# Loading the first two chunks of X by columns, and running the first piece of K ahead of the other turns

## The chip, the cores and the metric

The kernel runs on one core of a Trainium2 chip. Times are device microseconds (us) of that core. The engines are TensorE (PE; its weight loads are listed as PEld), VectorE (DVE), ScalarE (ACT), GpSimd (POOL) and SyncE (SP). DMAs are issued here from SP and from ACT. A time without a profile is the median over several executions; a profile is one execution, with times counted from its first instruction.

## What is computed

X has 2048 rows (S) of 640 features (D), in bfloat16. The result mixes two blocks with a gate per row:

```python
g = _sigmoid((x * gate_w).sum(-1, keepdims=True))
a = _A_ref(x, A_wqkv, A_wo)               # linear attention, 32 heads of 20
b = _B_ref(x, B_w1, B_w2, B_w3, B_w4)     # layernorm, gelu, shifts, MLP of 1728
return g * a + (1 - g) * b
```

The part that the change touches is the start of the attention block: `k = x @ wqkv[:, 640:1280]`, then `phi(k)`, for all rows, and with it the gate's sum `x * gate_w`, which the kernel computes as one more column of the same matrix product.

## The kernel before

X is cut into 16 chunks of 128 rows, its 640 features into 5 pieces (`dc`) of 128. A matmul of K for a chunk needs X transposed: `xT[:, dc, rows]` is the stationary operand and `wk_sb[:, dc, ...]`, one fifth of K's weights, the moving one. K's 640 outputs are taken in two halves (`hf`) of 320, each in its own bank of a PSUM pair, and each sums over the five `dc`. Half 1 has 321 columns: the last is the gate's, so that the gate's logit comes out beside K. So a chunk takes ten matmuls of K.

The schedule is written out by hand: each engine runs its instructions in the order in which the program lists them. The kernel's body is a sequence of stages: K for all chunks, Q, the products of phi(K) with X, two layer norms and the MLP. The change is in the first of them.

From chunk 2 on, X arrives already transposed by seven transposing loads that SP issues (L125). For chunks 0 and 1 that would come too late. They are loaded as they are (`load_x`, L122), and PE turns them itself: a matmul of a 128x128 block of `x_sb` with the identity (`turn`, L217) writes the turned block to PSUM, and a copy (L219), on DVE for pieces 0 and 1 and on ACT for pieces 2 to 4, brings it to `xT`.

The order of the issues at the start is: on SP chunk 0, chunk 1, K's weights 1 and 3, then the transposing loads; on ACT the gate's weights (`g5`, L131), then K's weights 0, 2 and 4 (L128), and then a table load and a first Exp (L208).

PE begins with filler matmuls (`warmup`, L204) on a constant, whose results nobody reads. The gate's weights arrive as five rows (`g5`), are copied into a zeroed square (`g5z`, L207), turned by one matmul of 5 columns (L210) and cast into the column `wk_sb[:, :, D]` (L212). Then come chunk 0's five turns, a filler, chunk 1's turns of pieces 1 and 0, K's piece 0 for chunk 0 (two matmuls, L191), chunk 1's other three turns, K's piece 0 for chunk 1, and the other four pieces of K for both chunks, sixteen matmuls. After each chunk ACT copies the gate's logit (L195) and takes the exponential (L183), and DVE ends phi (L184, L185). Chunks 2 to 15 follow with ten matmuls each.

Four PSUM pairs exist: `warm` and `tp` take the turns, and `kps[0]` and `kps[1]` the K sums of chunks 0 and 1. Fillers write to the second bank of `kps[1]`.

Of the kernel before, what the change touches and what calls it, by code (L numbers as in the profile page):

```python
# [7 lines left out]
ACT = mybir.ActivationFunctionType  # L8
# [8 lines left out]
def kernel(  # L17
# [13 lines left out]
    nc = tc.nc  # L31
    P = 128
    S, D = A_x.shape[1], A_x.shape[2]
# [3 lines left out]
    TS = 512  # L37
    NT = S // TS
    CPT = TS // P
    DC = D // P  # L40
# [12 lines left out]
    x2 = A_x.rearrange("b s d -> (b s) d")  # L53
# [14 lines left out]
    def pair():  # L68
        return ps.tile([P, 2, 512], F32, name="pp")


    x_sb = const.tile([P, NCH, D + 16], BF16)
# [15 lines left out]
    ident = const.tile([P, P], BF16)  # L88
    g5 = const.tile([DC, P], BF16)
    g5z = const.tile([P, P], BF16)  # L90
# [7 lines left out]
    gate = const.tile([P, NCH], F32)  # L98
# [12 lines left out]
    wk_sb = st1.tile([P, DC, D + 16], BF16)  # L111
    gT = wk_sb
    xT = st1.tile([P, DC, S], BF16)
# [5 lines left out]
    sp, aq, gq = nc.sync, nc.scalar, nc.gpsimd  # L119

    def load_x(c0, c1, q=sp):
        q.dma_start(x_sb[:, c0:c1, 0:D], x2[c0 * P:c1 * P, :].rearrange("(c p) d -> p c d", p=P))  # L122

    def load_xT(c0, c1):
        sp.dma_start_transpose(xT[:, :, c0 * P:c1 * P], x2[c0 * P:c1 * P, :])  # L125

    def load_wk(q, dc):
        q.dma_start(wk_sb[:, dc, 0:D], A_wqkv[dc * P:(dc + 1) * P, D:2 * D])  # L128

    load_x(0, 1)  # L130
    aq.dma_start(g5[:], gate_w.rearrange("(c p) -> c p", p=P))  # L131
    load_x(1, 2)
    load_wk(aq, 0)
    load_wk(sp, 1)
    load_wk(aq, 2)
    load_wk(sp, 3)
# [1 line left out]
    for c0, c1 in ((2, 3), (3, 4), (4, 6), (6, 8), (8, 10), (10, 12), (12, 16)):  # L138
        load_xT(c0, c1)
# [44 lines left out]
        nc.vector.tensor_scalar(e[:, 0:n], e[:, 0:n], 1.0, 1e-6, op0=ALU.min, op1=ALU.add)  # L184
        nc.vector.scalar_tensor_tensor(dst, src, 0.0, ev, op0=ALU.max, op1=ALU.add)  # L185

    def k_mm(pt, c, dcs, first=0, last=DC - 1):
        for dc in dcs:
            for hf in range(2):
                n = HD + hf  # L190
                nc.tensor.matmul(pt[:, hf, 0:n], lhsT=xT[:, dc, c * P:(c + 1) * P],  # L191
                                 rhs=wk_sb[:, dc, hf * HD:hf * HD + n], start=(dc == first), stop=(dc == last))
# [5 lines left out]
    warm, tp = pair(), pair()  # L198
    kps = [pair(), pair()]
    one = nc.const_aps.tensor(1.0, (P, TS), BF16)  # L200

    def warmup(n, w=TS, pt=kps[1]):
        for i in range(n):
            nc.tensor.matmul(pt[:, 1, 0:w], lhsT=one[:, 0:P], rhs=one[:, 0:w], start=True, stop=True)  # L204

    nc.vector.memset(g5z[:], 0.0)
    nc.vector.tensor_copy(g5z[0:DC, :], g5[:])  # L207
    nc.scalar.activation(gate[:, 0:1], one[:, 0:1], ACT.Exp)  # L208
    warmup(5)
    nc.tensor.matmul(kps[0][:, 0, 0:DC], lhsT=g5z[:], rhs=ident[:, 0:DC], start=True, stop=True)  # L210
    warmup(1, P)
    nc.vector.tensor_copy(wk_sb[:, :, D], kps[0][:, 0, 0:DC])  # L212

    def turn(c, dcs, pt, copy):
        a, n = min(dcs), len(dcs)
        for dc in dcs:
            nc.tensor.matmul(pt[:, 0, (dc - a) * P:(dc - a + 1) * P], lhsT=x_sb[:, c, dc * P:(dc + 1) * P],  # L217
                             rhs=ident[:], start=True, stop=True)
        copy(xT[:, a:a + n, c * P:(c + 1) * P], pt[:, 0, 0:n * P].rearrange("p (c s) -> p c s", c=n))  # L219

    turn(0, (1, 0), tp, nc.vector.tensor_copy)
    turn(0, (2, 3, 4), warm, nc.scalar.copy)
    warmup(1, TS)
    turn(1, (1, 0), tp, nc.vector.tensor_copy)
    k_mm(kps[0], 0, (0,))
    turn(1, (2, 3, 4), warm, nc.scalar.copy)
    k_mm(kps[1], 1, (0,))
    for dc in range(1, DC):
        for c in range(2):
            k_mm(kps[c], c, (dc,))  # L230
    for c in range(2):
        k_evac(kps[c], c)
    for c in range(2, NCH):
        pt = pair()
# [515 lines left out]
```

## Time and profile before

| what | us |
|---|---|
| median of 3 runs | 261.5 (261.31 to 261.77) |
| the profiled execution | 260.77 |
| its span, first to last instruction | 259.1 |
| PE busy | 254.2 (98%) |
| DVE busy | 147.6 (57%) |
| ACT busy | 108.0 (42%) |
| POOL busy | 32.5 (13%) |
| first filler on PE | 0.83 |
| first turn of X on PE | 3.19 |
| first matmul of K on PE | 4.54 |

Matmuls overlap each other: one starts while the one ahead of it is still draining. So a row's busy time and mean duration are longer than the time that a matmul adds, and the difference between the starts of two neighbours is the better measure. The brackets at the end of a timeline row tell how long the engine was idle ahead of it, and what ended that.

### The profile page before, as it was taken

The numbers are of one execution on the slowest core, as the hardware profiler recorded it, in microseconds if no ns is written. First come the engines' busy times: TensorE is split into PE (matmuls) and PEld (weight loads), VectorE is DVE, ScalarE is ACT, GpSimd is POOL, SyncE is SP. The second block draws the span as 40 slices with busy tenths as digits, with TensorE's granted clock in tenths as the row PEclk, the third lists the DMA queues.
The fourth block names the chain that finished last, engine by engine and source line by source line (L and its number), as shares of the span: only waits on it lengthen the run. The fifth ranks groups of instructions, "written<-read, shape, count | busy, mean of one in ns | idle before, by whom it ended". The sixth has DMA issues, their size and how long they took to land.

```text
span 259.1 us, 4189 instructions
## 1 busy us (share of the span) xinstructions
PE 254.2 (98%) x1624; PEld 150.1 (58%) x1647; DVE 147.6 (57%) x274; ACT 108.0 (42%) x168; POOL 32.5 (13%) x86
## 2 busy tenths in 40 slices
PE   8999999999999999999999999999999999999995
PEld 4777555688854644565464566464565555465553
DVE  2588778799999987687300497500288600125132
ACT  3555544375797447431352323343321343342100
POOL 4000040023411230041000131000132000000000
PEclk9999999999999999999999999999999999999999
DMA  7999998015571887943011023212022411211011
GB/s 198 213 186 371 347 265 280 7 34 123 126 116 39 131 163 218 315 122 76 3 41 41 20 65 84 78 32 50 20 53 72 101 23 41 59 29 59 17 52 52
DMA packets 57358, 27.98 MB, mean 108 GB/s; under 512 B 45394, under 2 KB 56442, under 8 KB 57338
## 3 DMA queue, kind: packets, MB, share of 16 engines
q1 hardware_dynamic: 56896, 27.22, 42.4%
q10 hardware_dynamic: 442, 0.49, 0.5%
q8 instruction: 13, 0.21, 0.4%
q14 instruction: 7, 0.06, 0.1%
HBM read 12.86 MB, written 3.47 MB: 63 GB/s over the span
## 4 chain that ended last, share of the span: by engine, by line
PE 98%; issue 1%; DVE 0%
PE pp L572 21%; PE pp L611 16%; PE pp L191 9%; PE pp L522 8%; PE pp L341 8%; PE pp L553 8%; PE pp L396 8%; PE pp L243 8%; PE pp L647 5%; PE pp L204 1%; PE pp L582 1%; PE pp L603 1%; PE pp L217 0%; PE pp L452 0%; PE pp L429 0%
## 5 line engine op out<-in xcount | busy, mean ns | idle before, releaser
L572 PE MATMUL pp<-lnxT,w_sb 128*128 128x512 bf16 x249 | 59.8, 379 | 0.6
L574 ACT ACTIVATE h<-pp 128x1024 bf16<-128x1024 f32 (+1 forms) x28 | 26.9, 962 | 56.0 <-PE pp L572 56.0
L611 PE MATMUL pp<-h,w_sb 128*128 128x512 bf16 (+1 forms) x228 | 42.4, 343 | 0.3
L572 PEld LDWEIGHTS <-w_sb 128*128 128x128 bf16 x260 | 25.2, 98 | 26.9
L525 DVE TENSOR_TENSOR x<-pp,x_sb 128x640 f32<-128x640 f32 x16 | 13.1, 816 | 41.0 <-PE pp L522 41.0
L611 PEld LDWEIGHTS <-w_sb 128*128 128x128 bf16 x234 | 22.7, 98 | 19.5 <-issue 1.0
L183 ACT ACTIVATE e<-pp 128x640 bf16<-128x640 f32 (+1 forms) x26 | 21.4, 827 | 9.6 <-PE pp L243 9.6
L304 POOL TENSOR_SCALAR rstd<-mv 128x1 f32<-128x1 f32 (+2 forms) x22 | 9.1, 415 | 127.9 <-DVE mv L310 126.9
L559 DVE SCALAR_TENSOR_TENSOR x<-pp,gate,x 128x640 f32<-128x640 f32 x16 | 14.1, 882 | 18.2 <-PE pp L553 12.6
L553 PE MATMUL pp<-m_sb,pqT 128*128 128x320 bf16 x160 | 24.3, 299 | 0.0
L522 PE MATMUL pp<-w_sb,hsT 128*128 128x320 bf16 x160 | 23.9, 299 | 0.0
L191 PE MATMUL pp<-wk_sb,xT 128*128 128x320 bf16 (+1 forms) x160 | 22.6, 303 | 0.0
L341 PE MATMUL pp<-x_sb,pk 128*128 128x320 bf16 (+1 forms) x160 | 22.0, 300 | 0.0
L243 PE MATMUL pp<-xT,hsT 128*128 128x512 bf16 x98 | 21.6, 379 | 0.1
L341 PEld LDWEIGHTS <-pk 128*128 128x128 bf16 x160 | 18.8, 117 | 3.2
L522 PEld LDWEIGHTS <-hsT 128*128 128x128 bf16 x160 | 15.6, 98 | 8.3 <-issue 0.4
L553 PEld LDWEIGHTS <-pqT 128*128 128x128 bf16 x160 | 15.7, 98 | 7.7
L624 DVE SCALAR_TENSOR_TENSOR oc<-pqT,omg,x 128x640 bf16<-128x640 bf16 x12 | 10.5, 878 | 16.7 <-DMA pqT<-hx 16.7
L191 PEld LDWEIGHTS <-xT 128*128 128x128 bf16 x160 | 15.8, 100 | 6.1
L396 PE MATMUL pp<-lnxT,w_sb 128*128 128x512 bf16 x77 | 17.9, 379 | 0.2
L243 PEld LDWEIGHTS <-hsT 128*128 128x128 bf16 x100 | 11.8, 118 | 9.7
L305 POOL TENSOR_TENSOR rstd<-rstd,mhalf 128x1 f32<-128x1 f32 (+2 forms) x22 | 16.7, 761 | 1.8
(93 smaller groups left out, 248.8 us busy)
## 6 DMA issues: line engine op xcount, KB each, us to landing
x_sb<-in_A_x_dram SPq DMA_DIRECT2D x1, 2240.0 KB
out_dram<-oc SPq DMA_DIRECT2D x14, 160.0 KB, 2.0
w_sb<-in_B_w_dram SPq DMA_DIRECT2D x1, 2160.0 KB, 17.0
w_sb<-in_B_w_dram SPq DMA_DIRECT2D x1, 2080.0 KB, 8.6
hsT<-in_A_wqkv_dram SPq DMA_DIRECT2D x1, 800.0 KB, 6.1
m_sb<-in_A_wqkv_dram SPq DMA_DIRECT2D x1, 800.0 KB, 12.1
w_sb<-in_B_w_dram SPq DMA_DIRECT2D x1, 800.0 KB, 11.5
m_sb<-m_dram SPq DMA_DIRECT2D x1, 800.0 KB, 4.3
```

The costliest lines, as they stand in the source:

```text
L183: nc.scalar.activation(ev, src, ACT.Exp)
L191: nc.tensor.matmul(pt[:, hf, 0:n], lhsT=xT[:, dc, c * P:(c + 1) * P], rhs=wk_sb[:, dc, hf * HD:hf * HD + n], start=(dc == first), stop=(dc ...
L243: nc.tensor.matmul(pt[:, t % 2, :], lhsT=wq_sb[:, dc, :].rearrange("p (m j) -> p j m", j=DC)[:, j], rhs=xT[:, dc, t * TS:(t + 1) * TS], st ...
L305: nc.gpsimd.tensor_tensor(out_ap, out_ap, mhalf[:, 0:out_ap.shape[1]], op=ALU.pow)
L341: nc.tensor.matmul(pt[:, hf, 0:HD + hf], lhsT=w, rhs=x_sb[:, c, hf * HD:(hf + 1) * HD + hf], start=(c == 0), stop=(c == NCH - 1))
L396: nc.tensor.matmul(pt[:, i, :], lhsT=w, rhs=lnxT[t][:, dc, :], start=(dc == 0), stop=(dc == DC - 1))
L522: nc.tensor.matmul(pt[:, hf, 0:HD], lhsT=hsT[:, fc, 2 + c * P:2 + (c + 1) * P], rhs=w2_sb[:, fc, hf * HD:(hf + 1) * HD], start=(fc == 0), ...
L553: nc.tensor.matmul(pt[:, hf, 0:HD], lhsT=pqT[:, j, c * P:(c + 1) * P], rhs=m_sb[:, j, hf * HD:(hf + 1) * HD], start=(j == 0), stop=(j == D ...
L559: nc.vector.scalar_tensor_tensor(x1, pt[:, :, 0:HD], gate[:, c:c + 1], x1, op0=ALU.mult, op1=ALU.add)
L572: nc.tensor.matmul(pt[:, k, :], lhsT=w3_sb[:, dc, fc * P:(fc + 1) * P], rhs=lnT[:, dc, :], start=(dc == 0), stop=(dc == DC - 1))
L574: nc.scalar.activation(h2[:, 2 * i * TS:(2 * i + n) * TS], pt[:].rearrange("p h e -> p (h e)")[:, 0:n * TS], ACT.Gelu_apprx_tanh)
L611: nc.tensor.matmul(dst, lhsT=w4_sb[:, fc, d * P:(d + 1) * P], rhs=st[t]["h2"][:, fc * TS + a:fc * TS + b], start=False, stop=(fc == FF - 1))
```

## The change

Chunks 0 and 1 of X are no longer loaded one after the other. A first transfer on SP brings features 0 to 127 of both chunks (64 KB), and a second one, on ACT, features 128 to 639 of both (256 KB). K's weights 0 move from ACT to SP, behind the first transfer.

PE's order follows: after four fillers (five before) it turns piece 0 of both chunks, runs two fillers, then half 0 of K's piece 0 for both chunks. The gate's weights are now turned behind that, into `warm` and not `kps[0]`, and g5z is copied behind the first turns' copy. Then come the turns of piece 1 of both chunks, half 1 of K's piece 0, the turns of pieces 2 to 4 of chunk 0 (copied by ACT) and of chunk 1 (now copied by DVE, through `tp`). The other sixteen K matmuls keep their order. The turns and the K matmuls are as many as before, and so are the DMAs.

```diff
+    def load_x01(q, a, b):
+        q.dma_start(x_sb[:, 0:2, a:b], x2[0:2 * P, a:b].rearrange("(c p) d -> p c d", p=P))
...
-    load_x(0, 1)
+    load_x01(sp, 0, P)
     aq.dma_start(g5[:], gate_w.rearrange("(c p) -> c p", p=P))
-    load_x(1, 2)
-    load_wk(aq, 0)
+    load_wk(sp, 0)
+    load_x01(aq, P, D)
     load_wk(sp, 1)
     load_wk(aq, 2)
     load_wk(sp, 3)
...
-    def k_mm(pt, c, dcs, first=0, last=DC - 1):
+    def k_mm(pt, c, dcs, hfs=(0, 1), first=0, last=DC - 1):
         for dc in dcs:
-            for hf in range(2):
+            for hf in hfs:
...
     nc.vector.memset(g5z[:], 0.0)
+    nc.scalar.activation(gate[:, 0:1], one[:, 0:1], ACT.Exp)
+    warmup(4)
+
+    def turn_mm(cs, dcs, pt):
+        for i, (c, dc) in enumerate([(c, dc) for dc in dcs for c in cs]):
+            nc.tensor.matmul(pt[:, 0, i * P:(i + 1) * P], lhsT=x_sb[:, c, dc * P:(dc + 1) * P],
+                             rhs=ident[:], start=True, stop=True)
+
+    def turn_copy(cs, dcs, pt, copy):
+        a, d, m, n = min(cs), min(dcs), len(cs), len(dcs)
+        copy(xT[:, d:d + n, a * P:(a + m) * P], pt[:, 0, 0:m * n * P].rearrange("p (d s) -> p d s", d=n))
+
+    turn_mm((0, 1), (0,), tp)
+    turn_copy((0, 1), (0,), tp, nc.vector.tensor_copy)
+    warmup(1)
+    warmup(1, 2 * P)
     nc.vector.tensor_copy(g5z[0:DC, :], g5[:])
-    nc.scalar.activation(gate[:, 0:1], one[:, 0:1], ACT.Exp)
-    warmup(5)
-    nc.tensor.matmul(kps[0][:, 0, 0:DC], lhsT=g5z[:], rhs=ident[:, 0:DC], start=True, stop=True)
-    warmup(1, P)
-    nc.vector.tensor_copy(wk_sb[:, :, D], kps[0][:, 0, 0:DC])
...
-    turn(0, (1, 0), tp, nc.vector.tensor_copy)
-    turn(0, (2, 3, 4), warm, nc.scalar.copy)
-    warmup(1, TS)
-    turn(1, (1, 0), tp, nc.vector.tensor_copy)
-    k_mm(kps[0], 0, (0,))
-    turn(1, (2, 3, 4), warm, nc.scalar.copy)
-    k_mm(kps[1], 1, (0,))
+    for c in range(2):
+        k_mm(kps[c], c, (0,), (0,))
+    nc.tensor.matmul(warm[:, 0, 0:DC], lhsT=g5z[:], rhs=ident[:, 0:DC], start=True, stop=True)
+    nc.vector.tensor_copy(wk_sb[:, :, D], warm[:, 0, 0:DC])
+    turn_mm((0, 1), (1,), tp)
+    turn_copy((0, 1), (1,), tp, nc.vector.tensor_copy)
+    for c in range(2):
+        k_mm(kps[c], c, (0,), (1,))
+    turn_mm((0,), (2, 3, 4), warm)
+    turn_copy((0,), (2, 3, 4), warm, nc.scalar.copy)
+    turn_mm((1,), (2, 3, 4), tp)
+    turn_copy((1,), (2, 3, 4), tp, nc.vector.tensor_copy)
     for dc in range(1, DC):
```

## The prediction, on record before the result

> **What bounds the kernel now.** First the page's busy table and its chain that ended last.
>
> ```profile
> PE 254.2 (98%) x1624; PEld 150.1 (58%) x1647; DVE 147.6 (57%) x274; ACT 108.0 (42%) x168; POOL 32.5 (13%) x86
> ...
> PE 98%; issue 1%; DVE 0%
> ```
>
> TensorE (PE) is busy from end to end. So a change at the front is worth what it moves the moment at which PE starts chunk 2 of K; from there the stream is the same. Second, the chain in order of time, for the front alone.
>
> ```profile
> 0.83 2.29 PE pp L204 x5
> 3.12 0.14 PE pp L210
> 3.27 0.13 PE pp L204
> 3.40 0.53 PE pp L217 x5
> 3.93 0.43 PE pp L204
> 4.36 0.39 PE pp L217 x2
> 4.75 0.53 PE pp L191 x2
> 5.28 0.32 PE pp L217 x3
> 5.60 21.69 PE pp L191 x158
> ```
>
> L204 is filler, L217 the turns of X, L191 the matmuls of K. Chunks 0 and 1 need 10 turns and 20 K matmuls. Third, how long these take, from the timeline of PE in small windows.
>
> ```profile
> 5.08 0.53 PE L217 MATMUL pp<-ident,x_sb 128*128 128x128 bf16 x3
> 5.39 0.47 PE L191 MATMUL pp<-wk_sb,xT 128*128 128x320 bf16 x1
> ...
> 5.39 1.05 PE L191 MATMUL pp<-wk_sb,xT 128*128 128x320 bf16 x5
> ...
> 6.01 2.34 PE L191 MATMUL pp<-wk_sb,xT 128*128 128x321 bf16 x16
> ```
>
> Spacing counts, not duration. Before about 5.8 us two K matmuls take 0.53 us (4.54 to 5.08), 0.267 each, and three turns 0.32, 0.107 each. From 6.01 sixteen K matmuls cover 2.34 less the last one's tail (0.30 long, spaced 0.136): 0.136 each. So PE runs at half speed until about 5.8 us and at full speed behind it, though the page's PEclk row says 9 throughout and so doesn't show this. Chunk 2's first K matmul starts 16 x 0.136 behind 5.88, at 8.06 us: the mark that the change must move.
>
> Fourth, what the front waits for: the answers for the transfers in small windows, the vector engine's (DVE's) timeline, and the tile view of x_sb.
>
> ```profile
> x_sb<-in_A_x_dram SPq DMA_DIRECT2D x1, 160.0 KB, 2.2
> ...
> x_sb<-in_A_x_dram SPq DMA_DIRECT2D x1, 160.0 KB, 3.1
> wk_sb<-in_A_wqkv_dram ACTq DMA_DIRECT2D x1, 160.0 KB, 3.1
> ```
>
> ```profile
> 2.66 0.36 DVE L207 COPY g5z<-g 5x128 bf16<-5x128 bf16 x1 [1.67 <-DMA g<-in_gate_w_dram]
> 3.30 0.18 DVE L212 CAST wk_sb<-pp 128x5 bf16<-128x5 f32 x1 [0.28 <-PE pp L210]
> 3.65 0.42 DVE L219 CAST xT<-pp 128x256 bf16<-128x256 f32 x1 [0.16 <-PE pp L217]
> ```
>
> ```profile
>   DMA x_sb<-in_A_x_dram: 0.6, 1
> ```
>
> Chunk 0 of X, issued at 0.79, lands at 3.0; chunk 1, issued at 1.24, at 4.3, and PE's weight loads wait 0.6 us for it; K's first weights, issued at 1.38, land at 4.5, just when the first K matmul wants them (4.54). PE itself is uncovered only from 2.92 to 3.08 and from 4.15 to 4.35, 0.36 us together.
>
> **The change part by part.** The sum is against the profiled execution: 260.77 us, 259.1 of span and 1.7 around it. The three timed runs have a median of 261.5, 0.73 above it, so I take differences from the profile and add them to 261.5.
>
> *The loads.* The same bytes, the same number of issues on each queue (four on SP ahead of the transposing loads, four on ACT ahead of its table load), so chunk 2's xT and the table load keep their times. What moves is the order.
> The first transfer (two chunks, 128 features, 64 KB in 256 rows of 256 B) has no row. From below: g's 256 B rows were there at 2.6. From above, if rows and not bytes are paid, 256 rows take as long as both old loads, 4.3. The window answer has 252 GB/s at 7.0 to 8.0, where the transposing loads move 256 B packets, against 315 at 4.5 to 5.0, so small rows are not paid per row; I take 3.0, chunk 0's own.
> K's first weights go from ACT's second place to SP's second. That place landed at 4.3, with 160 KB ahead of it; now 64 KB are ahead, and 96 KB less at the 202 to 234 GB/s of 2.0 to 3.0 is 0.4 us: 3.9. Bounds 3.5 and 4.5.
> The rest of X (256 KB) takes ACT's second place, which landed at 4.5 with 160 KB. 96 KB more, at half of some 310 GB/s (two queues share, windows of 3.0 to 5.0), are 0.6; the smaller transfer ahead gives up to 0.4 of it back. Bounds: 4.3 (chunk 1's landing) and 5.3 (at ACT's own step from its second to its third landing, 4.5 to 5.9 for 160 KB, 96 KB are 0.8). I take 4.85, between the two sums 4.7 and 5.1.
> ACT's later weights slip behind it, by up to 0.6: the third, issued at 1.78, landed 4.1 later at 5.9, and is wanted at about 6.6; the fourth, 6.7, is wanted at about 7.7. Both covered, the third by 0.1 at worst.
>
> *PE's order.* Taken away: one filler of 512 (0.43) and fillers of 128 and 512; added: fillers of 512 and 256 (0.43 and 0.21). These lie in waits. Step by step:
> Four fillers end at 2.54. First turns at 3.05 and 3.16, the second ends 0.31 later; DVE's copy follows by 0.04 and takes 0.42: 3.51 to 3.93. The fillers cover PE from 3.27 to 3.91.
> Two K matmuls of half 0, from 4.0 (copy and weights both there): 0.53, to 4.53. Here the change gains: in the old order no K matmul ran before 4.54.
> The gate's matmul at 4.55; in the old trace its cast was done 0.40 behind its start (3.08 to 3.48), so 4.95. The copy of g5z, which now waits behind the first turn's copy on DVE (0.36, 3.93 to 4.29), is hidden by the K pieces. The second turns' copy now queues behind the cast; it has to wait for X anyway.
> X's rest at 4.85: turns 4.90 to 5.11; K's half 1 (cast long done) 5.11 to 5.64; three turns of chunk 0, 5.64 to 5.91 with the clock opening at 5.8 as before; chunk 1's three share a bank pair with the second turns, whose copy is done at 5.78 (5.32, plus 0.04, plus 0.42): 5.91 to 6.07.
> Sixteen K matmuls at 0.136: 2.18, so chunk 2 starts at 8.25. Their copies: ACT's 128x384 took 0.46, so 6.58 against a use at 6.61. DVE's 128x384 is new: between 0.42 (its 128x256) and 0.63 (by size); 0.55 ends at 6.8 against a use at 6.88. If it took 0.63 the stall is just 0.05.
> Sum: 8.25 against 8.06, +0.19 us. Two K matmuls gained cold time (0.53), but the rest of X lands 0.55 behind the old chunk 1, with eight turns behind it instead of five (0.16 to 0.32). That the first half of the work is at half speed cuts both ways: work moved from behind 5.8 to before it pays double, and a wait before 5.8 costs only half as much in full-speed work. Forecast 261.7.
>
> **The rivals.**
> *The clock opens later.* In the old trace it opened 5.0 us after the first filler, with 0.36 us uncovered in between. The new order leaves 0.5 (2.54 to 3.05), 0.1 and 0.3 (4.6 to 4.9), 0.9 in all. If busy time is what counts, it opens 0.55 later; each later microsecond costs 1 minus 0.136/0.267, that is 0.49: +0.27 more, 262.0. If a gap makes the count start again, 5.0 us behind 4.9, all sixteen are cold: 16 x 0.131 = +2.1, 263.8. For it: more gaps just where it matters. Against it: the old gaps did not stop it. Somewhere between, typically +1.0: 262.7.
> [...]
> *The rest of X, or the first rows, late.* With the rest at 5.3 the same steps end at 8.6 (+0.55, 262.05). With the first rows at 4.3, K's pieces start at 5.3, and chunk 2 at 9.2 (+1.15, 262.65). For it: 256 KB on one queue, 256 rows each. Against: the rates above.
> *Faster.* The place is the copies between X's landing and chunk 1's turns: rest at 4.3, first rows at 2.6, and the clock open by 4.6 in the runs. Then half 1 runs 4.65 to 4.92, chunk 0's turns to 5.08, chunk 1's wait for the copy until 5.23, and chunk 2 starts at 5.39 + 2.18 = 7.57: -0.49, 261.0. It decides on the clock: with 5.8 the same arrivals give 8.07, no gain. For it: the timed runs differ from the profile by more than this. Against it: the trace has 5.8.
>
> **How the numbers follow.** Forecast 0.45 (own range 261.4 to 262.05), clock later 0.23, data late 0.19, faster 0.13. A measurement of this kernel tells about 0.2% (0.52 us) from no change: 260.98 to 262.02. Faster: 0.11 of its rival. Slower: 0.20 of the clock, 0.17 of the late data, 0.03 of the forecast, 0.40. The same: 0.49. The range goes from the faster rival's 261.0 to 262.8, which takes in the late data and the middle of the clock's; about 0.15 is left out.
>
> **What would show it.** The first turns near 3.05 and two K matmuls before 4.6; PE waiting for x_sb near 4.85; chunk 2's first K matmul near 8.25; the spacing of K falling from 0.267 to 0.136 near 5.8. The prediction is wrong if that fall comes at 7 or later, if X's rest lands outside 4.3 to 5.3, or if a K matmul stalls on its weights behind 6.6.

## The result, and the profile after

The changed kernel takes 263.22 us (median of 6 executions, 262.42 to 263.48) against 261.4 for the kernel before (6 executions, 260.67 to 261.79). The ratio is 1.0064, with a 95% interval of 1.0044 to 1.0084: slower by 0.6%, some 1.7 us. The profiled execution took 263.31 us, its span 261.6 against 259.1.

The chain that ended last, in order of time, for the front of the changed kernel (start, duration, what):

```profile
1.30 3.34 DMA wk_sb<-in_A_wqkv_dram
4.63 0.04 issue
4.68 0.69 PE pp L194 x2
5.37 0.01 PE pp L229
5.37 0.23 PE pp L215 x2
5.60 0.04 issue
5.64 0.70 PE pp L194 x2
6.34 0.64 PE pp L215 x6
6.98 22.84 PE pp L194 x156
```

(L194 is K, L215 the turns, L229 the gate's matmul, L207 the fillers.) The old chain was PE alone from 0.83 us on. Now its first piece is a transfer: K's first weights, issued at 1.30, land at 4.63, and no work of PE stands ahead of that in the chain. The timeline of PE shows the hole:

```profile
2.69 0.40 PE L215 MATMUL pp<-ident,x_sb 128*128 128x128 bf16 x2
2.88 0.85 PE L207 MATMUL pp<-const-bfloat16-1.0 128*128 128x512 bf16 x2
4.68 0.69 PE L194 MATMUL pp<-wk_sb,xT 128*128 128x320 bf16 x2 [0.95 <-DMA wk_sb<-in_A_wqkv_dram]
5.16 0.21 PE L229 MATMUL pp<-ident,g5z 128*128 128x5 bf16 x1
```

The last filler's columns are through at 3.52 (it starts at 3.30 and has 256), so PE waits 1.16 us by starts, 0.95 in the profile's count, which includes the drain. Then the spacing of K's matmuls, from timeline windows further on:

```profile
7.31 1.81 PE L194 MATMUL pp<-wk_sb,xT 128*128 128x320 bf16 x6
...
10.31 1.93 PE L194 MATMUL pp<-wk_sb,xT 128*128 128x320 bf16 x13
```

Six K matmuls from 7.31 cover 1.81 less a tail of 0.47, 0.267 each: half speed still. Thirteen from 10.31 cover 1.93 less 0.30, 0.136 each. The spacing falls at 10.2 us; in the kernel before it fell at 5.9. Of the sixteen K matmuls that start at 6.78, twelve go at 0.267, one at 0.19 and three at 0.136, so chunk 2 starts at 10.59 and not at 8.06. That is 2.53 us, and the spans differ by 2.5: what comes behind chunk 2 is as before. The profile of before was one of its faster executions (260.77 of a median of 261.4), which is why the traces differ by more than the medians.

How much of it is which? Had the clock opened at 5.8 here, PE's steps from 5.64 would be: second K matmul of half 1 at 5.87 to 6.0, the six turns to 6.33 (0.056 each at full speed, as e6_half_fill below has them; the copy that the last three wait for ends at 6.07, before they start), sixteen K matmuls to 8.51. So by this estimate the late data are worth some 0.45 us and the late clock some 2.1 in this pair of executions. The experiments test that.

### The profile page after: what moved, and what is told of

The parts are those of the page before. It is cut to its first block, busy times and chain, and to the rows that moved or that the text cites. A ratio compares the mean times of both kernels' runs of the same rounds, so it can differ in the third digit from the quotient of the medians.

```text
span 261.6 us, 4188 instructions
## 1 busy us (share of the span) xinstructions
PE 255.7 (98%) x1623; PEld 150.6 (58%) x1646; DVE 148.0 (57%) x275; ACT 107.7 (41%) x167; POOL 32.8 (13%) x86
## 4 chain that ended last, share of the span: by engine, by line
PE 97%; DMA 1%; issue 1%; SPq 0%; DVE 0%
PE pp L583 21%; PE pp L622 16%; PE pp L194 9%; PE pp L533 8%; PE pp L352 8%; PE pp L564 8%; PE pp L407 8%; PE pp L254 8%; PE pp L658 5%; DMA wk_sb<-in_A_wqkv_dram 1%; PE pp L593 1%; PE pp L614 1%; PE pp L463 0%; PE pp L440 0%; PE pp L215 0%
## 5 line engine op out<-in xcount | busy, mean ns | idle before, releaser
L194 PE MATMUL pp<-wk_sb,xT 128*128 128x320 bf16 (+1 forms) x160 | 24.4, 317 | 1.0 <-DMA wk_sb<-in_A_wqkv_dram 1.0
L194 PEld LDWEIGHTS <-xT 128*128 128x128 bf16 x160 | 16.4, 103 | 8.6 <-issue 1.2
```

## Experiments

Two theories. **The gap**: PE stands idle too long in its first microseconds and its clock opens later for that. **The data**: K's weights and X's rest come later, and that alone is the loss. Ratios are to the kernel before, timed on the same chip in the same rounds, with 95% intervals.

### Fill the gap: e1_fill

```diff
     turn_copy((0, 1), (0,), tp, nc.vector.tensor_copy)
-    warmup(1)
-    warmup(1, 2 * P)
+    warmup(3)
+    warmup(2, 2 * P)
```

> The changed kernel with 1.07 us more filler matmuls (two of 512 columns, one of 256) behind the first turns, so that TensorE's gap from 3.52 to 4.68 us closes; nothing else moves. Theory (the gap makes TensorE's clock open late): the K matmuls' spacing falls from 0.267 to 0.136 some 3 us earlier than at 10.1, near 5.8 to 7.5; chunk 2 of K starts at 8.5 to 9.0 and not at 10.59; time 261.8 to 262.2. Rival (the later transfers alone make the loss, and the clock opens when it will): no change from the changed kernel, chunk 2 at 10.6, 263.2.

Measured: 261.25 us (260.90 to 261.71, 10 executions), ratio 1.0012 (0.9995 to 1.0030). PE's timeline, front and K:

```profile
3.01 1.91 PE L207 MATMUL pp<-const-bfloat16-1.0 128*128 128x512 bf16 x5
4.72 0.74 PE L194 MATMUL pp<-wk_sb,xT 128*128 128x320 bf16 x2
...
6.81 3.44 PE L194 MATMUL pp<-wk_sb,xT 128*128 128x320 bf16 x24
```

K starts at 4.72, 0.04 later than in the changed kernel, and K's first weights land at 4.66 here: the data are no earlier. But all 24 matmuls from 6.81 are at full spacing (3.44 less 0.30, over 23). Matmuls that nobody reads took away about 0.5 of the 0.6% (0.4, if the changed kernel's second measurement, 1.0050 in e9_after_again, is taken). The kernel before took 260.82 in these rounds and not 261.4, so ratios compare: the theory's 261.8 to 262.2 are 1.0015 to 1.003, just above what came, and the rival's 263.2, 1.007, is out. What is left of the loss, 0.12%, can't be told from nothing.

### Open a gap in the kernel before: e2_before_gap

```diff
-    warmup(5)
+    warmup(3)
...
-    warmup(1, TS)
     turn(1, (1, 0), tp, nc.vector.tensor_copy)
```

> The kernel before with three fillers of 512 less (two of the first five, and the one between the two chunks' turns), so that TensorE stands idle from about 2.1 to 3.1 and from 3.7 to 4.35; loads, turns, K matmuls and what they wait for stay. Theory: the clock opens a good deal later than 5.8, up to 10; 16 K matmuls cost up to 0.13 more each; time 262.4 to 263.4. Rival (fillers do nothing for the clock): 261.4, as before.

Measured: 261.91 us (261.31 to 263.95), ratio 1.0043 (1.0018 to 1.0067).

```profile
2.88 0.19 PE L210 MATMUL pp<-ident,g5z 128*128 128x5 bf16 x1 [0.61 <-DVE g5z L207]
...
5.44 2.35 PE L191 MATMUL pp<-wk_sb,xT 128*128 128x321 bf16 x8
7.85 1.53 PE L191 MATMUL pp<-wk_sb,xT 128*128 128x320 bf16 x10
```

Less work, more time. K's first matmul even starts earlier than before (4.37 against 4.54, the second chunk of X landed early in that execution), but eight matmuls from 5.44 cover 2.35 (0.267 each), and full speed comes at 7.85. With old loads and old order the gap alone costs about 0.4%; the theory's 262.4 to 263.4 are 1.004 to 1.008 of 261.4, so this is at their lower end, and the rival's 1.000 is out. Both directions agree: the gap is the larger part of the loss. One of these ten executions, 263.95, lies far from the rest, and no profile caught it.

### Where K's first weights stand: e3_swap, e4_wk0_first, e7_cols256, e13_rest_first

The changed kernel's loads, in other orders or cuts; PE's order is its own in all four.

```diff
 # e3_swap
-    load_wk(sp, 0)
-    load_x01(aq, P, D)
+    load_x01(sp, P, D)
+    load_wk(aq, 0)
 # e4_wk0_first
-    aq.dma_start(g5[:], gate_w.rearrange("(c p) -> c p", p=P))
-    load_wk(sp, 0)
-    load_x01(aq, P, D)
+    load_wk(aq, 0)
+    load_x01(sp, P, D)
+    aq.dma_start(g5[:], gate_w.rearrange("(c p) -> c p", p=P))
 # e7_cols256
-    load_x01(sp, 0, P)
+    load_x01(sp, 0, 2 * P)
...
-    load_x01(aq, P, D)
+    load_x01(aq, 2 * P, D)
 # e13_rest_first
-    aq.dma_start(g5[:], gate_w.rearrange("(c p) -> c p", p=P))
-    load_wk(sp, 0)
-    load_x01(aq, P, D)
+    load_x01(aq, P, D)
+    load_wk(sp, 0)
+    aq.dma_start(g5[:], gate_w.rearrange("(c p) -> c p", p=P))
```

> The changed kernel with the second places of the two queues exchanged: the rest of X second on SP, K's first weights second on ACT as in the kernel before. If the place on SP makes K's first weights late (4.63 where 3.9 was expected), they land at about 4.5 still, since ACT's second place gave 4.5 before; the gap in front of K's first piece stays and so does the late clock: 263.0 to 263.3. The rest of X lands at 4.6 to 5.0 and not 5.13. If instead the slow packets of 2.4 to 3.5 come with K's weights themselves, the rest of X lands at 4.3 to 4.5 there.

Measured: two groups of executions, 261.00 to 261.14 (four) and 262.47 to 263.78 (six); ratio 1.0039 (1.0002 to 1.0076). K's first weights landed at 4.88 and X's rest at 5.12. Both are late whichever queue and place they have, so it is neither the place on SP nor K's weights themselves. The two groups were not expected, and come back below.

> The changed kernel with 256 features in the first transfer (rows of 512 B) and 384 in the second. In the changed kernel the DMA engines moved only 95 to 104 GB/s from 2.5 to 3.5 us, where the kernel before had 202 to 353, and K's first weights landed at 4.63. If that slump comes from rows of 256 B, it goes, and K's first weights land at 4.1 to 4.4 in spite of 64 KB more ahead of them. If it comes with the number of rows, or with the start of the second transfer whatever is ahead of it, it stays, and they land at 4.6 or later.

One execution: K's first weights at 4.28 in spite of 64 KB more ahead of them, full speed at 8.0, 262.09 us. That spoke for the rows' size; but e10 below has the same loads, and there they landed at 4.60. So rows of 512 B do not settle it.

> The changed kernel with K's first weights first on ACT, the rest of X second on SP and the gate's weights second on ACT. K's first weights then land at 2.9 to 3.4, ahead of the first turns' copy (3.55), so that K's first two matmuls run at 3.6 and the gap of 1.16 us goes without a filler; what is left is a wait of about 0.4 to 0.8 for the rest of X (4.5 to 5.0). Theory of the gap: the clock opens at 5.8 to 7.5, chunk 2 starts at 8.1 to 8.8, 261.4 to 262.0. Rival of the later transfers: the rest of X decides, 262.5 or more.

Measured: 262.49 us (261.72 to 262.95), ratio 1.0046 (1.0022 to 1.0069). The hole has moved, not gone: with K's weights under way beside them (309 GB/s from 2.5 to 3.0, 363 to 3.5) the first features of X land at 3.53 where they had landed at 2.64, and PE is idle from 2.49 to 3.57; K starts at 4.48 and full speed comes at 8.7. The expectation that a smaller hole would be left missed that.

> The changed kernel with the gate's weights behind the rest of X on ACT, so that ACT's queue has data to move from its first issue (0.79) on, as it had in e4_wk0_first, where 309 and 363 GB/s were moved from 2.5 to 3.5 us. If the slump of the changed kernel (95 and 104 GB/s there) comes from one queue alone having work while ACT's large transfer starts late (3.0), it goes: 250 GB/s or more from 2.5 to 3.5, the rest of X at 4.4 or earlier, K's first weights at 4.2 or earlier, the gap in front of K's first piece under 0.7, time 261.0 to 262.2. If it comes from the rows of 256 B, the slump stays, K's first weights land at 4.6 or later, and the time stays at 262.5 to 263.3.

Measured: 262.39 us (261.37 to 263.07), ratio 1.0041 (1.0010 to 1.0073). The windows of the changed kernel, then of e13 (stretch and length, busy time by engine, PEclk, DMA share, GB/s):

```profile
2.50:3.00 0.50, 0.50 (x4) 0.32 (x4) 0.00 (x0) 0.15 (x1) 0.42 (x2) 1.00 1.01 95
3.00:3.50 0.50, 0.50 (x3) 0.03 (x1) 0.38 (x2) 0.50 (x1) 0.36 (x2) 1.00 0.41 104
```

```profile
2.50:3.00 0.50, 0.19 (x1) 0.00 (x0) 0.00 (x0) 0.15 (x1) 0.42 (x2) 1.00 1.08 340
3.00:3.50 0.50, 0.10 (x2) 0.11 (x3) 0.00 (x0) 0.50 (x1) 0.36 (x2) 1.00 1.09 386
```

The rows of 256 B are first in both. With ACT's large transfer issued at 0.79 the slump is gone, as it was in e4 (309 and 363), and K's first weights land at 4.31, not 4.63. So the slump is not the rows' size. It was gone in the two kernels where both queues had large transfers from the start; in the changed kernel ACT spends its first 0.58 us on the issue of the gate's five rows, its large transfer is issued at 1.40, and that transfer's first packet starts at 3.04. Why SP's queue alone moved just 95 GB/s at 2.5 to 3.0, where it moved 202 in the kernel before, nearly alone (ACT's first large packet starts at 2.87 there), stays open. K's first weights came 0.1 later and the time 0.1% higher than expected: with 340 GB/s moved from 2.5 to 3.0, and not 95, the first turns start at 3.40, not 2.69, and the hole is there (2.49 to 3.40).

### How the opening falls: e6_half_fill, e8_before_again, e9_after_again

```diff
 # e6_half_fill
-    warmup(1)
+    warmup(2)
     warmup(1, 2 * P)
```

> The changed kernel with one filler of 512 (0.43 us) in the gap in front of K's first piece, so that some 0.7 us of 1.16 are left. If the clock opens at the end of a stretch of some 3.4 us that is busy by more than a share between 0.66 (the busiest such stretch so far that did not open it) and 0.89 (the least busy one that did), the worst stretch is now busy by some 0.63 and most others by more than 0.7: two groups of times, as e3_swap has them (261.0 to 261.1 and 262.5 to 263.8), with more in the early one; median 261.5 to 262.5. Rival (the opening is delayed in proportion to the idle time): one group, half way between e1_fill and the changed kernel, 1.004.

Measured: 260.92 and 262.64, 263.52, 263.53 (four executions, median 263.08), ratio 1.0080 (1.0052 to 1.0107). One early and three late, not one group half way, as the rival had it; but four executions are few, and more of them were late than expected, so half a filling bought nothing that these four show. In the profiled one, the early one, the gap in front of K was 0.37 us, with K's first weights there at 4.47, and full speed came at 5.4. How long the gap was in the three late ones is not known.

> The kernel before, unchanged, profiled once more. If the stretch by which the clock opens runs free of the kernel's start, the spacing of K's matmuls falls from 0.267 to 0.136 at another time than 5.8, anywhere from 4.5 to 8, and chunk 2 of K starts at 7.6 to 9.2. If the opening is tied to the kernel's own matmuls, it is at 5.6 to 6.0 again.

One execution: full speed at 6.2, 260.96 us; chunk 2 at 8.25. Neither 5.6 to 6.0 nor far from it: the spacing alone does not decide, and the clock's record below says more.

> The changed kernel, unchanged, in more executions. If the opening is a matter of where free-running stretches of some 3.4 us fall against a gap of 1.16 us, nearly all executions miss one and a few do not: most at 262.4 to 263.8, one in ten or so near 261, and the profile opens anywhere from 7.4 to 10.8. If the opening is a fixed delay behind the gap, all executions lie within 0.5 us of each other and the profile opens at 10.1 again.

Measured: 262.46 us (260.85 to 263.54, 12 executions), ratio 1.0050 (1.0024 to 1.0075). Four lie at 260.85 to 261.38, the other eight at 262.03 to 263.54; the profile's full speed came at 9.5 (10.2 in the first). Not a fixed delay. Early executions are more frequent than the one in ten that was expected. No profile caught one, so whether K's weights came earlier in them is not shown.

The table has for each profile the longest idle stretch of PE ahead of its full speed (from the starts of the matmuls and their columns), the start of the first matmul at full spacing, and that execution's time. The column between is the clock itself: the trace keeps a record of the granted clock, and this is where its first entry, full speed, begins. (The page's PEclk row counts only what stands in that record, and nothing stands in it ahead of this entry; e12's trace has no entry at all.)

| kernel | longest gap, us | clock record opens, us | full speed from, us | profiled execution, us |
|---|---|---|---|---|
| e11_dense_fill | 0.08 | 4.50 | 4.5 | 260.34 |
| e10_cols256_dense | 0.41 | 4.75 | 4.8 | 260.49 |
| e12_before_filled | 0.08 | none | 5.3 | 260.49 |
| e6_half_fill | 0.40 | 4.82 | 5.4 | 260.92 |
| e5_fill_gate | 0.35 | 5.49 | 5.6 | 261.42 |
| before | 0.20 | 5.81 | 5.9 | 260.77 |
| before again (e8) | 0.31 | 6.14 | 6.2 | 260.96 |
| e1_fill | 0.34 | 6.73 | 6.8 | 261.71 |
| e2_before_gap | 0.82 | 7.84 | 7.9 | 261.65 |
| e7_cols256 | 0.68 | 7.98 | 8.0 | 262.09 |
| e4_wk0_first | 1.08 | 8.57 | 8.7 | 262.47 |
| e13_rest_first | 0.91 | 8.70 | 8.8 | 262.49 |
| e3_swap | 1.23 | 9.09 | 9.1 | 262.98 |
| after again (e9) | 1.07 | 9.43 | 9.5 | 263.04 |
| after | 1.16 | 10.09 | 10.2 | 263.31 |

Every profile with no gap over 0.41 reached full speed by 6.8, every one with a gap of 0.68 or more at 7.9 or later. Over a range of 5.7 us the time follows the opening: from e11 to the changed kernel 2.97 us, 0.52 per microsecond, next to the 0.49 that the two spacings give (1 minus 0.136/0.267). Loads and order show beside it, but less: e5_fill_gate took 0.65 us more than the kernel before, though its clock opened 0.3 us earlier.

The record shows more. From its first entry on, full speed stands in it for 252.59 us in ten profiles, the kernel before and the changed one among them, and for 256.00 in four, those that opened first (e11, e10, e6 and e5). These differ by 3.41 us, and they are 74 and 75 times that. So it is an estimate, from these two durations alone, that the clock changed in steps of 3.41 us in these profiles; no run tests the step. (The expectation of e6 assumed some 3.4 before a run had shown it.) The openings do not keep one distance from the kernel's start: the kernel before opened at 5.81 and at 6.14, the changed one at 10.09 and at 9.43, with the first filler at 0.83 in all four. If the opening ends a step, that step and the one ahead of it can be read. Counting the columns of the matmuls at the speed of the moment, an estimate: in all fourteen profiles with a record, PE was busy for 0.77 (e6) or more of the 3.41 us that ended at the opening, and for 0.71 (e7) or less of the 3.41 us ahead of those. (In seven of them that earlier stretch began before PE's first matmul.) In e6 the later stretch had 0.8 us of idle time, in two gaps of 0.40 and 0.37; in e7 the earlier one had 1.0 us, in gaps of 0.68 and 0.32. That an idle share between the two decides is not shown by any run.

The groups of one kernel lie some 2 us apart (e3_swap: 261.00 to 261.14 and 262.47 to 263.78), near the 1.7 that an opening 3.41 us later would cost by an estimate from the two spacings (0.49 per microsecond).

### A closer order: e5_fill_gate, e10_cols256_dense, e11_dense_fill, e12_before_filled

```diff
 # e5_fill_gate: e1_fill, and the gate's matmul among the fillers
     turn_copy((0, 1), (0,), tp, nc.vector.tensor_copy)
-    warmup(1)
-    warmup(1, 2 * P)
+    warmup(2)
     nc.vector.tensor_copy(g5z[0:DC, :], g5[:])
-    for c in range(2):
-        k_mm(kps[c], c, (0,), (0,))
     nc.tensor.matmul(warm[:, 0, 0:DC], lhsT=g5z[:], rhs=ident[:, 0:DC], start=True, stop=True)
     nc.vector.tensor_copy(wk_sb[:, :, D], warm[:, 0, 0:DC])
+    warmup(1)
+    warmup(2, 2 * P)
+    for c in range(2):
+        k_mm(kps[c], c, (0,), (0,))
```

> The fillers of e1_fill, and the gate's matmul of 5 columns moved from behind K's half 0 to between the fillers, so that its cast is long done when K's half 1 wants it. In e1_fill TensorE stood idle there from 5.49 to 5.74. Theory (what e1_fill still loses on the kernel before is late data and this wait): the gap goes, chunk 2 of K starts 0.12 to 0.25 earlier at the same opening of the clock, ratio to the kernel before 1.000 to 1.001 where e1_fill has 1.0012. Rival (the wait is hidden behind the turns): as e1_fill.

Measured: 261.46 us (261.02 to 261.67), ratio 1.0020 (1.0003 to 1.0036): not better than e1_fill.

```profile
4.21 0.19 PE L226 MATMUL pp<-ident,g5z 128*128 128x5 bf16 x1
4.26 1.01 PE L207 MATMUL pp<-const-bfloat16-1.0 128*128 128x512 bf16 x3
5.07 0.65 PE L194 MATMUL pp<-wk_sb,xT 128*128 128x320 bf16 x2
```

The wait in front of half 1 went, and two others came: the gate's matmul waits for DVE's copy of g5z (PE idle from 3.88 to 4.21), and the fillers behind it then end after K's weights are there (4.94). Chunk 1's last turns wait for the bank pair again, from 6.10 to 6.34. A miss.

```diff
 # e10_cols256_dense: the loads of e7_cols256, and
+    nc.vector.tensor_copy(g5z[0:DC, :], g5[:])
     nc.scalar.activation(gate[:, 0:1], one[:, 0:1], ACT.Exp)
-    warmup(4)
+    warmup(5)
+    nc.tensor.matmul(warm[:, 0, 0:DC], lhsT=g5z[:], rhs=ident[:, 0:DC], start=True, stop=True)
+    warmup(1, P)
+    nc.vector.tensor_copy(wk_sb[:, :, D], warm[:, 0, 0:DC])
...
     turn_copy((0, 1), (0,), tp, nc.vector.tensor_copy)
+    turn_mm((0, 1), (1,), warm)
+    turn_copy((0, 1), (1,), warm, nc.vector.tensor_copy)
     warmup(1)
     warmup(1, 2 * P)
-    nc.vector.tensor_copy(g5z[0:DC, :], g5[:])
     for c in range(2):
-        k_mm(kps[c], c, (0,), (0,))
-    nc.tensor.matmul(warm[:, 0, 0:DC], lhsT=g5z[:], rhs=ident[:, 0:DC], start=True, stop=True)
-    nc.vector.tensor_copy(wk_sb[:, :, D], warm[:, 0, 0:DC])
-    turn_mm((0, 1), (1,), tp)
-    turn_copy((0, 1), (1,), tp, nc.vector.tensor_copy)
-    for c in range(2):
-        k_mm(kps[c], c, (0,), (1,))
+        k_mm(kps[c], c, (0,))
     turn_mm((0,), (2, 3, 4), warm)
 # e11_dense_fill: e10, and
     warmup(1, 2 * P)
+    warmup(1, 3 * P)
```

> Rows of 512 B in the first transfer (256 features of both chunks), the gate's matmul back among the first fillers, four turns behind the first transfer, and all four K matmuls of piece 0 before the other turns, with 1.07 us of fillers fewer gaps: no idle time over 0.4 us on TensorE. If the gap is what cost the time, no execution falls in the late group and the time is that of the kernel before within 0.2%: ratio 0.998 to 1.002; the forecast for chunk 2 is 8.1 at an opening of 5.8. If the column loads as such cost time, 1.003 or more.

Measured: 260.88 us (260.27 to 261.49, 12 executions), ratio 0.9989 (0.9973 to 1.0005). K's first weights land at 4.60, X's rest at 4.94, both later than their counterparts in the kernel before (4.49 and 4.30), and yet:

```profile
4.64 0.74 PE L194 MATMUL pp<-wk_sb,xT 128*128 128x320 bf16 x4 [0.21 <-DMA wk_sb<-in_A_wqkv_dram]
5.22 0.50 PE L219 MATMUL pp<-ident,x_sb 128*128 128x128 bf16 x6
5.56 4.69 PE L194 MATMUL pp<-wk_sb,xT 128*128 128x320 bf16 x33
```

All from 5.56 is at full spacing, chunk 2 starts at 7.77, and no execution falls in the late group. Loading by columns costs nothing that was measured where PE stays busy.

> e10_cols256_dense with one filler more, of 384 columns (0.32 us), in front of K's first matmul, where TensorE still stood idle from 4.23 to 4.64. If what e10 has left to gain is early opening of the clock, the slow end of its times goes (261.0 to 261.5) and the ratio is 0.997 to 0.999; if its remaining time is the transfers', it stays at 0.999.

Measured: 260.99 us (260.30 to 261.53), ratio 0.9999 (0.9988 to 1.0011). The filler did not take the slow end away: a miss.

```diff
 # e12_before_filled: the kernel before, and
     warmup(5)
+    warmup(1, P)
...
     warmup(1, TS)
+    warmup(1, 3 * P // 2)
```

> The kernel before with its own two small gaps filled (a filler of 128 behind the first five, one of 192 behind the one between the turns; 0.27 us). Both gaps lie far below the idle share that kept the clock shut (0.28 or more), so by the theory nothing changes: ratio 0.999 to 1.001. If any idle time delays the clock in proportion, 0.27 us earlier, 0.13 us or 0.9995, which this can't tell from the theory; a ratio below 0.998 would speak against a threshold.

Measured: 260.85 us (260.49 to 263.62, 12 executions), ratio 1.0012 (0.9988 to 1.0037): nothing, as the theory has it. But two of its executions took 263.58 and 263.62, and one of the 28 of the kernel before, timed beside e1 to e4, 263.71. No profile caught one of those. They look like another kind than the late groups above: their mean granted clock was 0.993, where it was 0.999 or 1.0 in every other execution, the late ones of the changed kernel included. What lowered it is not known. One more execution of the kernel before, timed beside e13, took 263.41 with a clock of 1.0. By the theory these kernels have no gap that could do it; a late transfer could make one, but that was not seen. So both kinds stay open.

No version beats the kernel before by more than a measurement can tell.

## Why the prediction was wrong

The forecast was 261.7 (no measurable change) with a range to 262.8; measured were 263.22. Slower by over 0.2% had a chance of 0.40, and the mechanism that happened was its first rival, with 0.23.

- **"the clock opening at 5.8 as before"**: this step failed. It was taken over from one execution of the old kernel as if it were a property of the chip, when in these profiles it moved with PE's idle time: full speed by 6.8 us where no gap was over 0.41, at 7.9 or later where one was 0.68 or more. By the clock's record it opened at 5.81 and 6.14 in the kernel before, and at 10.09 and 9.43 in the changed one; a fall at 7 or later was one of the prediction's own signs of being wrong. The rival that named it took a typical price of 1.0 above the sum; the runs give 0.4 to 0.5% for the gap (e1), 0.4% in the kernel before (e2), 1.0 to 1.4 us, and 2.1 us in the profiled pair. Its harsher branch, an opening 5.0 us behind the last gap, at 9.9, and 263.8, came near by luck: from the last gap of over 0.2 us to the opening it is 4.4 us here, 3.1 in e4 and 1.0 in e1. The argument against that rival, "the old gaps did not stop it", held for gaps of 0.2 us only; in e8 one of 0.31 did not stop it either.
- **K's first weights at 3.9 (bounds 3.5 and 4.5)**: 4.63. This is the step that made the gap. The working took the rate of the kernel before at 2.0 to 3.0 (202 to 234 GB/s) for an order in which SP's queue works alone longer and ACT's large transfer starts later (first packet at 3.04 against 2.87); the windows have 95 and 104. Outside its bounds, and the second place where a number of the old kernel was carried into another order. The same loads gave 4.66, 4.94, 4.47 and 4.74 in e1, e5, e6 and e9.
- **The idle time of PE, 0.9 us in pieces of 0.5, 0.1 and 0.3**: one piece of 1.16, and 0.20, 0.07 and 0.25. The sum, 0.9, was little over half of the 1.68; the prediction did see that gaps are what the clock hangs on, and priced them against arrivals that were too early.
- **First features at 3.0 (from 2.6)**: 2.64, at the lower bound, and 2.78 to 2.85 in e1, e3, e5, e6 and e9; 256 rows of 256 B were not what was late. Of no use, since K's weights were what was late.
- **X's rest at 4.85 (4.3 to 5.3)**: 5.13, inside.
- **"the gate's cast long done"**: its matmul slid with K's pieces to 5.16, the cast ended at 5.59, and half 1 waited 0.25 us for it. Small, and hidden in the forecast by the early K weights.
- **DVE's 128x384 copy, 0.55**: 0.557. The ACT copy 0.48 against 0.46. The later K weights stalled nothing, as said.
- **The sum with the clock at 5.8, +0.19**: worked again with the measured arrivals it is +0.45, 0.17%; e1_fill, with the gap filled, measures 0.12% (0 to 0.30%). The data part was right in kind and small; the loss was in the other term.

## What to carry to other kernels

In the first microseconds TensorE's matmuls ran at half speed here (0.267 us for one of K, against 0.136), until 4.5 to 6.8 us in the profiles with no gap over 0.41 and until 7.9 to 10.2 in those with one of 0.68 or more. So a wait there was paid twice: once as the wait, and again as all the work that still ran at half speed behind it (e2_before_gap, 0.4% with less work). Fillers in such a wait are part of the schedule. When an order is changed, look for the first arrival that now has no work ahead of it, and fill to its latest landing, not to the expected one; and when a kernel's executions fall into groups, read the spacing of its matmuls in more than one profile before an early or late number is taken as given.

## What was not expected of the hardware

- A gap of 1.07 to 1.16 us among matmuls, at half speed and in the first 5 us, put off full speed by 3.6 to 4.3 us in the two profiles (9.5 and 10.2 against 5.9).
- One and the same program has executions some 2 us apart (e3_swap: 261.0 to 261.1 and 262.5 to 263.8).
- In the changed kernel SP's queue, alone behind a transfer of 64 KB, moved 95 GB/s from 2.5 to 3.0, and with the first packets of ACT's large transfer 104 from 3.0 to 3.5; in e13, with ACT's large transfer issued at 0.79, it was 340 and 386. In the kernel before SP's queue, with 183 of the 188 packets, moved 234 and 202 from 2.0 to 3.0, and why is open.
